# Attention and a two-layer MLP on one core: Winograd's running sums move into PSUM, and the down-projection lags by two periods

## The chip, the cores and the metric

The kernel runs on one core of a Trainium2 chip. The metric is device time of one execution in microseconds (us). Engines are named as in the profile: PE (TensorE), DVE (VectorE), ACT (ScalarE), POOL (GpSimd), SP (SyncE, which issues most DMAs). PEld is PE's weight load.

## The reference

```python
# q, k, v: (8, 8, 576, 64) float32; moe_w_in (512, 2048), moe_w_out (2048, 512)
scores = q @ k.T / 8
# heads 0-3: a query sees the 32 keys up to itself; heads 4-7: every 32nd key up to itself
attn = softmax(where(mask, scores, -1e9)) @ v
x = attn.transpose(0, 2, 1, 3).reshape(4608, 512)
out = (maximum(x @ w_in, 0) ** 2) @ w_out
```

## The kernel before, in words

Every float32 operand of a large matmul is split into a high part h and a rest l (both fp32r), and a product is three matmuls (hh, hl, lh). 4608 tokens are in 12 chunks of 384 (`TC`).

*Attention.* Heads 0-3 ("local") are done chunk by chunk on PE in `pair(c, pr)`: scores s (16 matmuls), minima on DVE (L268), exp on ACT (L275), scaling on ACT and POOL, transposes on DVE (L289), then o (16 matmuls). `STARTS` gives the half step at which each pair of heads begins. Heads 4-7 ("strided") use no PE: in `strided(c)` POOL multiplies (pq, L440; pp, L462) and DVE sums (L441, L463), with two buffers between them, and a softmax between the two halves (L446 to L453); results are transposed by DVE into `ring["s"]`. Their instructions are dealt out over the steps by `PACE` (units of work by step) in `advance`.

*First stage* (to 338 us): chunks 0 to 3 are multiplied plainly by `up` (L499) and `down` (L532), 64 steps. Meanwhile `combos` forms, for each of eight weight pieces p, the seven sums of 256 x 256 weight blocks that Winograd's form of Strassen's scheme needs, split into h and l, and stores them in DRAM (`scr`).

*Second stage*: the other 3072 tokens in six blocks m of 512, eight periods p each, period q = 8m + p. `up7(q)` forms two 128-row tiles of x @ w_in by seven products (1, 7, 2, 6, 4, 3, 5) of a weight sum (tiles ea, eb, streamed from `scr` by `stream`) and an operand op1 to op7 of 256 tokens, six matmuls of 256 columns each (L702). Running sums are kept by accumulating in three PSUM banks u and copying them by ACT to SBUF in between (`keep`, L716); three DVE adds join them into h (L730 to L732), which lies in SBUF. `square(q, h)` squares (L739, L740) and splits them (cast L741; rest L742, one tile on DVE, one on POOL) into g. `down7(q)` multiplies g by w_out into four PSUM banks yy, one for each 128 tokens, 24 matmuls of 512 columns (L758). It runs one period late, but for the last period of a block, whose `down7` runs right away. After it `split_x(m + 1)`, called ahead of that, has rewritten the seven operands from the ring: seven casts on ACT (L675), seven differences (L676; four on DVE, three on POOL) and four sums on DVE (L679, L680, L684, L686), in place in the ring.

The order on each engine is made by a list scheduler at build time, from the order of the code, dependencies and priorities; PE's order is fixed by `on_pe`. Each engine runs its own queue in order.

Of the kernel before, what the change touches and what calls it, by code (L numbers as in the profile page):

```python
# [18 lines left out]
STR = 32  # L19
# [3 lines left out]
P = 128  # L23
# [27 lines left out]
PACE = ((2, 0), (10, 104), (15, 104), (31, 328), (47, 604), (60, 952), (108, 2192), (140, 2812))  # L51

STARTS = {
    2: (8, 12), 3: (16, 20), 4: (22, 24), 5: (26, 28), 6: (32, 34),
    7: (40, 42), 8: (46, 48), 9: (50, 52), 10: (54, 56), 11: (62, 64),
# [62 lines left out]
def attn_moe(ctx: ExitStack, tc, qk_d, v_d, qk_p, v_p, f_s, q_s, k_s, v_s, w_in, w_out, masks, eye, out):  # L118
# [113 lines left out]
    done_to = {"split": 0, "l": 0, "s": 0}  # L232

    def into(kind, c, col, n):

        t0 = TC * (c - NCL) + col
        assert t0 + n - RING <= done_to["split"] <= t0, (kind, c, col, done_to)
        done_to[kind] += n
        return in_ring(c, col, n)


    def pair(c, pr):
# [10 lines left out]
        vr = buf(lpool, "v", 2 * NW * D, "vx", bufs=1)  # L253
        last["s"] = nc.sync.dma_start(out=vr, in_=v_d[c, pr])
# [5 lines left out]
        s_ps = [psum((3 + h) if c <= NCL + 1 else 1 + h, f"s{h}{u}") for h in range(2)]  # L260
        for w in range(NW):
            k0 = TC + wins[w][0]
            for h in range(2):
                rows = slice(D * h, D * (h + 1))
                last["mm"] = nc.tensor.matmul(s_ps[h][:QC, w * kw : (w + 1) * kw], qk[rows, w * QC : (w + 1) * QC], qk[rows, k0 : k0 + kw], start=True, stop=True)
# [6 lines left out]
        yield  # L272
        for h in range(2):
# [29 lines left out]
        else:  # L303
            for a, b, at in into("l", c, 0, TC):
# [110 lines left out]
    def strided(c):  # L415
        for b, i0, i1, col in ranges(c):
# [48 lines left out]
            if c >= NCL:  # L465
                for a in range(2):
                    for n0, n1, at in into("s", c, col, ni * STR):
# [49 lines left out]
    def down(c, j):  # L517
        gh, gl = g_tiles.pop((c, j))
# [10 lines left out]
        for t in range(NTT):  # L529
# [3 lines left out]
        if j == NFT - 1:  # L533
            for t in range(NTT):
# [88 lines left out]
    def combos():  # L623
        for p in range(NPER):
            hi, lo = wi[p]
            for i, at in ((0, 0), (2, 2 * P), (4, 6 * P)):
                nc.sync.dma_start(out=scr[p][:, i], in_=f32(pieces[p][:, :, at : at + 2 * P]))
            full = spare[:, :1024]
            for n, at in enumerate((512, 0)):
                sl = slice(at, at + 512)  # L630
                (nc.gpsimd if n else nc.vector).tensor_add(full[:, sl], f32(hi[:, sl]), f32(lo[:, sl]))
                yield
# [8 lines left out]
            for i, t in ((1, s3), (3, s2), (5, s4), (6, s1)):  # L641
                so = lpool.tile([P, 2, 2 * P], F32R, name=f"so{p}_{i}", tag="so", bufs=1)
                nc.scalar.copy(so[:, 0], t)
                nc.gpsimd.tensor_sub(so[:, 1], t, f32(so[:, 0]))  # L644
                nc.sync.dma_start(out=scr[p][:, i], in_=f32(so))
# [21 lines left out]
    def split_x(m):  # L667
        assert done_to["l"] >= 2 * min(TS * (m + 1), NT - NCL * TC) and done_to["s"] >= TS * (m + 1), (m, done_to)
        v, g = nc.vector, nc.gpsimd
# [3 lines left out]
        def split(nm, src, eng):  # L673
            t = opnd[nm]
            nc.scalar.copy(t[:, 0], src)  # L675
            eng.tensor_sub(t[:, 1], src, f32(t[:, 0]))  # L676

        split("1", b11, v)
        v.tensor_sub(b11, b12, b11)  # L679
        v.tensor_sub(b12, b22, b12)  # L680
        split("7", b12, v)
        split("2", b21, g)
        split("3", b22, v)
        v.tensor_sub(b22, b22, b11)  # L684
        split("6", b22, v)
        v.tensor_sub(b21, b21, b22)  # L686
        split("4", b21, g)
        split("5", b11, g)
        done_to["split"] = TS * (m + 1)
# [6 lines left out]
    def product(acc, e, x, start):  # L696
# [11 lines left out]
    def up7(q):  # L708
        e = entry.pop(q)
        x, y, a = (psum(i, f"u{i}_{q}") for i in range(3))  # L710
        vt = ring["v"]
# [298 lines left out]
```

## Time and profile before

| | |
|---|---|
| median of 3 runs | 950.7 us (950.64 to 954.09) |
| profiled execution, its span | 950.65 us, 948.8 us |
| PE, PEld busy | 93%, 82% |
| DVE, ACT, POOL busy | 72%, 55%, 70% |
| second stage on PE | 338.4 to 944.9 us |
| granted clock, mean | 0.974 |

Busy is the share of the span in which the engine had an instruction under way; it is a mean over stages. A wait is put down to the instruction whose semaphore came last. The chain of work that ended last is followed back from the last instruction.

### The profile page before, as it was taken

The page shows a single profiled execution, that of the slowest core. Times are in us where ns is not written, and L with a number is a line of the kernel's source. Part 1 is how long each engine was busy: PE and PEld are TensorE (multiplying, and loading weights), DVE is VectorE, ACT ScalarE, POOL GpSimd, SP SyncE. Part 2 cuts the span into 40 slices and gives each one's busy share as a digit, 9 for nine tenths or more (in the row PEclk, how much of TensorE's full clock was granted, in tenths as well). Part 3 has the DMA queues.
Part 4 walks back from the last instruction along what each step waited for, and adds up shares of the span by engine and source line. Part 5 has one row for each costly group of instructions (what it writes and reads, how often), then busy time and mean ns, then how long its engine had stood idle before and what let it go on. Part 6 is the DMA issues. An engine that isn't in the chain of part 4 may idle for free.

```text
span 948.8 us, 16167 instructions
## 1 busy us (share of the span) xinstructions
PE 883.6 (93%) x5587; PEld 776.5 (82%) x5587; DVE 682.9 (72%) x1776; ACT 518.5 (55%) x1334; POOL 661.8 (70%) x664
## 2 busy tenths in 40 slices
PE   8999999999999989997999599996999789999998
PEld 7888797887788878886888488885888578888997
DVE  5786779788888878787777977788767977453222
ACT  6998645455555545453655445563644644554443
POOL 3789787878676788797699688877889868321111
PEclk9999999999999999998999799997999899999999
DMA  9986523324264164663656265553755344545441
GB/s 358 389 295 194 191 76 108 115 101 144 89 229 160 37 219 139 210 242 120 225 180 216 103 211 179 197 186 108 236 198 196 109 165 161 196 156 200 159 152 45
DMA packets 46001, 165.93 MB, mean 175 GB/s; under 512 B 4768, under 2 KB 11552, under 8 KB 38240
## 3 DMA queue, kind: packets, MB, share of 16 engines
q1 hardware_dynamic: 45632, 164.58, 49.8%
q8 instruction: 44, 0.72, 0.3%
q10 hardware_dynamic: 288, 0.33, 0.1%
q14 instruction: 37, 0.30, 0.1%
HBM read 140.77 MB, written 24.12 MB: 174 GB/s over the span
## 4 chain that ended last, share of the span: by engine, by line
PE 44%; DVE 21%; POOL 16%; ACT 11%; issue 5%; DMA 3%; ACTq 0%; POOLq 0%; DVEq 0%
PE yy L758 19%; PE u L702 17%; POOL pp L462 5%; POOL pq L440 5%; DVE p_t L289 4%; PE y L532 3%; DVE op L676 3%; DVE sc L441 2%; PE h L499 2%; ACT e L275 2%; DMA scr<-so 2%; POOL w L209 2%; DVE qs L463 1%; POOL so L644 1%; ACT h L739 1%
## 5 line engine op out<-in xcount | busy, mean ns | idle before, releaser
L758 PE MATMUL yy<-w,g 128*128 128x512 f32 x864 | 226.5, 402 | 32.0 <-ACT g L741 21.8
L440 POOL TENSOR_TENSOR pq<-ks,qs 128x512 f32<-128x512 f32 (+2 forms) x192 | 209.1, 1109 | 33.6 <-DVE sc L441 30.0
L462 POOL TENSOR_TENSOR pp<-vs,sc 128x448 f32<-128x448 f32 (+10 forms) x192 | 197.3, 1054 | 47.5 <-DVE qs L463 24.5
L758 PEld LDWEIGHTS yy<-w,g 128*128 128x128 f32 x864 | 162.1, 193 | 70.5 <-ACT g L741 24.0
L499 PE MATMUL h<-x,w 128*128 128x384 f32 x768 | 148.1, 343 | 11.7 <-DVE gl L513 6.8
L702 PE MATMUL u<-op,ea 128*128 128x256 f32 x1152 | 150.3, 285 | 6.9 <-ACT ring L716 5.0
L702 PEld LDWEIGHTS u<-op,ea 128*128 128x128 f32 x1152 | 144.8, 191 | 14.5 <-ACT ring L716 7.5
L716 ACT COPY ring<-u 128x256 f32<-128x256 f32 x192 | 70.5, 371 | 153.5 <-PE u L702 152.1
L441 DVE TENSOR_REDUCE sc<-pq 128x8 f32<-128x512 f32 (+4 forms) x228 | 118.9, 533 | 47.1 <-POOL pq L440 44.8
L499 PEld LDWEIGHTS h<-x,w 128*128 128x128 f32 x768 | 135.2, 190 | 19.3 <-DVE gl L513 10.7
L463 DVE TENSOR_REDUCE qs<-pp 128x64 f32<-128x448 f32 (+11 forms) x192 | 106.5, 564 | 52.8 <-POOL pp L462 51.5
L532 PE MATMUL y<-w,gh 128*128 128x512 f32 x384 | 119.8, 396 | 0.5 <-POOL w L209 0.5
L702 PE MATMUL u<-op,eb 128*128 128x256 f32 x864 | 113.5, 284 | 5.1 <-ACT ring L716 4.7
L702 PEld LDWEIGHTS u<-op,eb 128*128 128x128 f32 x864 | 107.3, 192 | 7.3 <-ACT ring L716 7.3
L739 ACT ACTIVATE h<-h 128x512 f32<-128x512 f32 x96 | 58.9, 632 | 62.8 <-DVE h L731 62.3
L758 PE MATMUL yy<-w,op 128*128 128x512 f32 x288 | 86.0, 409 | 0.0
L532 PEld LDWEIGHTS y<-w,gh 128*128 128x128 f32 x384 | 71.8, 189 | 15.3 <-POOL w L209 0.8
L742 DVE TENSOR_TENSOR g<-h,g 128x512 fp32r<-128x512 f32 x48 | 55.9, 1165 | 36.6 <-ACT g L741 36.3
L742 POOL TENSOR_TENSOR g<-h,g 128x512 fp32r<-128x512 f32 x24 | 32.1, 1339 | 63.1 <-ACT g L741 63.0
L289 DVE STREAM_TRANSPOSE p_t<-e 32x128 f32<-32x128 f32 x240 | 72.1, 300 | 3.9 <-ACT e L281 1.0
L742 POOL TENSOR_TENSOR op<-h,op 128x512 fp32r<-128x512 f32 x24 | 36.3, 1513 | 55.2 <-ACT op L741 49.3
L532 PE MATMUL y<-w,gl 128*128 128x512 f32 x192 | 73.4, 394 | 0.0
(131 smaller groups left out, 1303.8 us busy)
## 6 DMA issues: line engine op xcount, KB each, us to landing
ea<-scr SPq DMA_DIRECT2D x48, 1024.0 KB, 5.1
eb<-scr SPq DMA_DIRECT2D x48, 768.0 KB, 5.9
scr<-so SPq DMA_DIRECT2D x32, 256.0 KB, 2.0
raw<-w_in SPq DMA_DIRECT2D x7, 1024.0 KB, 11.2
v<-v_d SPq DMA_DIRECT2D x24, 256.0 KB, 4.6
scr<-w SPq DMA_DIRECT2D x24, 256.0 KB, 5.7
y<-ysbb SPq DMA_DIRECT2D x24, 256.0 KB, 2.0
vs<-v_s SPq DMA_DIRECT2D x10, 576.0 KB, 4.1
```

Source lines behind the costliest of these rows:

```text
L289: nc.vector.transpose(out=p_t[h][STR * k : STR * (k + 1), :, STR * r : STR * (r + 1)], in_=ev[STR * r : STR * (r + 1), :, STR * k : STR * ...
L440: nc.gpsimd.tensor_mul(pv, kt[:, a : a + m, :], qt[:, i - i0 : i - i0 + 1, :].broadcast_to([P, m, D]))
L441: nc.vector.tensor_reduce(out=sc[:, i - i0, a : a + m], in_=pv, op=ALU.add, axis=AX.X)
L462: nc.gpsimd.tensor_mul(pv, vt[:, a : a + nd, :n], sc[:, il : il + 1, :n].broadcast_to([P, nd, n]))
L463: nc.vector.tensor_reduce(out=ot[:, il, a : a + nd], in_=pv, op=ALU.add, axis=AX.X)
L499: done = nc.tensor.matmul(ph[:, :TC], w[:, wsl], xx, start=n == 0, stop=n == 11)
L532: done = nc.tensor.matmul(y_ps[c][t], g[:, sl], w[:, wsl], start=j == 0 and k == 0, stop=j == NFT - 1 and k == 2)
L702: done = nc.tensor.matmul(acc, w, xx, start=start and n == 0, stop=n == 5, skip_group_check=not start)
L716: nc.scalar.copy(vt[:, i], src[:, :HS])
L739: nc.scalar.activation(h[o], h[o], AF.Relu)
L742: (nc.gpsimd if o else nc.vector).tensor_sub(gl, h[o], f32(gh))
L758: done = nc.tensor.matmul(y_ps[m][t], g[:, sl], w[:, wsl], start=p == 0 and o == k == 0, stop=p == NPER - 1 and o == 1 and k == 2)
```

## The change

Products now run in the order 1, 7, 2, 6, 5, 4, 3 in `period(q, ...)`. ACT copies the running sum x into the bank of h1 (first half, later second half) and of h2 (first half); products 2, 4 and 3 are accumulated by PE on top of what ACT wrote there, with no clearing start. DVE adds only product 7 (v7), once into h2 and once in place into h1. Relu, Square and the cast then work on the PSUM banks, and both rests are DVE's (`finish`). The four token tiles of a down-projection stand between the products: tile 0 behind product 7, tile 1 behind 6, tile 2 behind 4, tile 3 behind 3. They belong to period q - 2, at the ends of blocks too; the first two periods take the last two steps of the first stage, and two down-projections follow the last period. `sums_of_x(m)` forms the four operand sums on POOL into tiles of their own, a period ahead; `split_x(m)` does seven casts (ACT) and seven rests, all on POOL, at high priority.

In `combos` both halves of a weight sum are added by POOL (one was DVE's); the four stored sums rotate over three buffers instead of one, and positions 4 to 6 of `scr` change places. The v of a local pair is loaded after its scores. `PACE` and `STARTS` change by a few numbers.

```diff
-PACE = ((2, 0), (10, 104), (15, 104), (31, 328), (47, 604), (60, 952), (108, 2192), (140, 2812))
+PACE = ((2, 0), (10, 104), (15, 104), (31, 328), (47, 604), (60, 952), (106, 2192), (140, 2812))
-    2: (8, 12), 3: (16, 20), 4: (22, 24), 5: (26, 28), 6: (32, 34),
+    2: (8, 12), 3: (16, 20), 4: (22, 24), 5: (26, 28), 6: (32, 35),
...
 def combos():
-                (nc.gpsimd if n else nc.vector).tensor_add(full[:, sl], f32(hi[:, sl]), f32(lo[:, sl]))
+                nc.gpsimd.tensor_add(full[:, sl], f32(hi[:, sl]), f32(lo[:, sl]))
...
+    def sums_of_x(m):
+        t1, t2 = (pl.tile([P, TS], F32, name=f"t{i}_{m}", tag=tag) for i in (1, 2))
+        t3 = lpool.tile([P, TS], F32, name=f"t3_{m}", tag="so", bufs=1)
...
+        g.tensor_sub(t3, b22, b12)
+        g.tensor_sub(t1, b12, b11)
+        g.tensor_sub(t2, b22, t1)
+        g.tensor_sub(t4, b21, t2)
+        xsum[m] = {"1": b11, "7": t3, "2": b21, "6": t2, "5": t1, "4": t4, "3": b22}
+    def split_x(m):
+        for nm, src in xsum.pop(m).items():
+            t = opnd[nm]
+            with tc.high_priority():
+                nc.scalar.copy(t[:, 0], src)
+                nc.gpsimd.tensor_sub(t[:, 1], src, f32(t[:, 0]))
...
+    def finish(q, half, t):
+        gh, gl = (gs[4 * (q % 2) + 2 * half + i] for i in range(2))
+        nc.scalar.activation(t, t, AF.Relu)
+        nc.scalar.activation(t, t, AF.Square)
+        nc.scalar.copy(gh, t)
+        nc.vector.tensor_sub(gl, t, f32(gh))
+        return gh, gl
+    def period(q, downs, scores, outputs):
+        x, h1 = psum(0, f"x{q}"), psum(1, f"ha{q}")
+        product(first(x), e[0], opnd["1"], True)
+        with hp():
+            nc.scalar.copy(first(h1), first(x))
+        t7 = psum(3, f"t{q}")
+        product(first(t7), e[1], opnd["7"], True)
+        with hp():
+            nc.scalar.copy(v7, first(t7))
+        downs(0)
+        product(first(h1), e[2], opnd["2"])
+        product(first(x), e[3], opnd["6"])
+        with hp():
+            nc.scalar.copy(second(h1), first(x))
+        scores()
+        downs(1)
+        product(first(x), e[4], opnd["5"])
+        product(second(h1), e[5], opnd["4"])
+        h2 = psum(2, f"hb{q}")
+        with hp():
+            nc.scalar.copy(first(h2), first(x))
+            nc.vector.tensor_add(second(h2), first(x), v7)
+            nc.vector.tensor_add(second(h1), second(h1), v7)
+            g1 = finish(q, 0, h1)
+        downs(2)
+        outputs()
+        product(first(h2), e[6], opnd["3"])
+        downs(3)
+        with hp():
+            g2 = finish(q, 1, h2)
...
+    for q in range(NM * NPER + 2):
+        def downs(t, q=q):
+            if q >= 2:
+                down7(q - 2, t)
+            elif t < NTT:
+                on_pe(lambda: down(NCL - 1, NFT - 2 + q, t))
...
+        if p == NPER - 2 and m + 1 < NM:
+            sums_of_x(m + 1)
+        period(q, downs, lambda: scores(k), lambda: outputs(k))
```

How the change moves instructions, at three places. On PE, at the end of the second block (period 15; u are the up-projection's banks, yy1 the block's four output banks, w1_7 the w_out piece of period 15), before:

```order
L702 MATMUL u2_15_6287<-op43_4152,eb15_6066 128x256 x6
L702 MATMUL u0_15_6285<-op5_4153,eb15_6066 128x256 x6
L758 MATMUL yy1_0_5503<-w1_6_1231,g_4154 128x512 x6
L758 MATMUL yy1_1_5504<-w1_6_1231,g_4154 128x512 x6
L758 MATMUL yy1_2_5505<-w1_6_1231,g_4154 128x512 x6
L758 MATMUL yy1_3_5506<-w1_6_1231,g_4154 128x512 x6
L758 MATMUL yy1_0_5503<-w1_7_1282,g_4154 128x512 x3
L758 MATMUL yy1_0_5503<-w1_7_1282,op5_4153 128x512 x3
```

and after (x, t, ha, hb are the banks of the running sum, product 7, h1 and h2):

```order
L714 MATMUL hb15_6388<-op43_4127,eb15_6153 128x256 x6
L778 MATMUL yy1_3_5634<-w1_5_1103,op5_4128 128x512 x6
L714 MATMUL x16_6484<-op17_4125,ea16_6293 128x256 x6
L714 MATMUL t16_6493<-op17_4125,ea16_6293 128x256 x6
L778 MATMUL yy1_0_5631<-w1_6_1231,g_4129 128x512 x6
```

The tiles that need period 15's g (w1_7) stood right behind period 14's; now the next block's products start behind the last tile of period 13.

On DVE, in period 20, around the joining of the sums (sc<-pq are the strided reductions), before:

```order
L441 TENSOR_REDUCE sc9_3_6433<-pq9_3_14_0_6738 128x8
L730 TENSOR_TENSOR h1_20_7062<-u1_20_7059,ring_3198 128x256
L441 TENSOR_REDUCE sc9_3_6433<-pq9_3_14_8_6741 128x7
L731 TENSOR_TENSOR h1_20_7062<-u0_20_7058,ring_3198 128x256
L732 TENSOR_TENSOR h0_20_7061<-u2_20_7060,ring_3198 128x512
L441 TENSOR_REDUCE sc9_3_6433<-pq9_3_15_0_6744 128x8
```

and after:

```order
L443 TENSOR_REDUCE sc9_3_6455<-pq9_3_7_0_6460 128x8
L755 TENSOR_TENSOR hb20_7133<-x20_7079,ring_3182 128x256
L756 TENSOR_TENSOR ha20_7080<-ha20_7080,ring_3182 128x256
L443 TENSOR_REDUCE sc9_3_6455<-pq9_3_8_0_6463 128x8
L443 TENSOR_REDUCE sc9_3_6455<-pq9_3_8_8_6466 128x1
L725 TENSOR_TENSOR g_4129<-ha20_7080,g_4129 128x512
```

Three adds became two, both into PSUM; the strided attention stands about ten reductions further back against the same period.

On POOL, where the operands are rewritten for the fourth block (L742 are rests of g, pp products of the strided attention), before:

```order
L742 TENSOR_TENSOR g_4154<-h1_22_7365,g_4154 128x512
L462 TENSOR_TENSOR pp9_3_12_32_7055<-vs9_3_6429,sc9_3_6433 128x416
L462 TENSOR_TENSOR pp9_3_13_0_7200<-vs9_3_6429,sc9_3_6433 128x448
L462 TENSOR_TENSOR pp9_3_13_32_7203<-vs9_3_6429,sc9_3_6433 128x448
L283 TENSOR_TENSOR e110_0_7439<-e110_0_7439,rs10_0_7441 96x512
L462 TENSOR_TENSOR pp9_3_14_0_7206<-vs9_3_6429,sc9_3_6433 128x480
L676 TENSOR_TENSOR op26_4151<-spare_90,op26_4151 128x512
L462 TENSOR_TENSOR pp9_3_14_32_7209<-vs9_3_6429,sc9_3_6433 128x480
L462 TENSOR_TENSOR pp9_3_15_0_7212<-vs9_3_6429,sc9_3_6433 128x512
L676 TENSOR_TENSOR op5_4153<-ring_3198,op5_4153 128x512
```

and after (L689 to L692 are operand sums, L700 rests of operands):

```order
L464 TENSOR_TENSOR pp9_3_10_32_6946<-vs9_3_6451,sc9_3_6455 128x352
L689 TENSOR_TENSOR t3_3_7333<-spare_90,ring_3182 128x512
L691 TENSOR_TENSOR t2_3_7332<-spare_90,t1_3_7331 128x512
L700 TENSOR_TENSOR op43_4127<-spare_90,op43_4127 128x512
L464 TENSOR_TENSOR pp9_3_11_0_6949<-vs9_3_6451,sc9_3_6455 128x384
L464 TENSOR_TENSOR pp9_3_11_32_6952<-vs9_3_6451,sc9_3_6455 128x384
L700 TENSOR_TENSOR op17_4125<-t3_3_7333,op17_4125 128x512
L692 TENSOR_TENSOR ring_3182<-spare_90,t2_3_7332 128x512
L700 TENSOR_TENSOR op26_4126<-t2_3_7332,op26_4126 128x512
```

The rests of g left POOL; operand sums and all rests of operands came, each block's behind the strided products that complete its tokens. The rewriting begins about seven strided products earlier than it did (ahead of pp9_3_11 instead of behind pp9_3_14).

More of the change, by code (lines that the diff above doesn't have):

```diff
@@ L264, in pair @@
                 rows = slice(D * h, D * (h + 1))
-                last["mm"] = nc.tensor.matmul(s_ps[h][:QC, w * kw : (w + 1) * kw], qk[rows, w * QC : (w + 1) * QC], qk[rows, k0 : k0 + kw], start=True, stop=True)
+                last["mm"] = nc.tensor.matmul(s_ps[h][:QC, w * kw : (w + 1) * kw], qk[rows, w * QC : (w + 1) * QC], qk[rows, k0 : k0 + kw], start=not (late and w), stop=True, skip_group_check=late)
         for h in range(2):
@@ L528, in down @@
         wsl = slice(o * DM, (o + 1) * DM)
-        for t in range(NTT):
+        tiles = range(NTT) if only is None else (only,)
+        for t in tiles:
             sl = slice(t * P, (t + 1) * P)
@@ L694, in on_pe, with product @@
             last["pe"] = mm()
[L696 removed]
+    def product(acc, e, x, start=False):
         def mm():
```

198 lines of the change are left out of this document (79 added, 119 removed).

## The prediction

> **What bounds the kernel now.** I read the head of the page first, then the chain that ended last, then a table by stage.
>
> ```profile
> span 948.8 us, 16167 instructions
> PE 883.6 (93%) x5587; PEld 776.5 (82%) x5587; DVE 682.9 (72%) x1776; ACT 518.5 (55%) x1334; POOL 661.8 (70%) x664
> ```
>
> PE is busy 93%, so the question is where the other 65 us are. The profiled execution took 950.65 us, its span 948.8; the median of the runs is 950.7, so a sum made against the profile holds for the median too. The chain (start, length, what) shows what a down-projection with attention matmuls in it costs (first four rows), and an undisturbed period (last two):
>
> ```profile
> 367.33 1.39 PE yy L758 x6
> 368.72 0.81 PE o L298 x16
> 369.53 1.56 PE s L265 x16
> 371.09 4.31 PE yy L758 x18
> ...
> 397.43 5.03 PE u L702 x42
> 402.46 5.47 PE yy L758 x24
> ```
>
> Seven products take 5.03 us, the four token tiles of a down-projection 5.47: a period is 10.5 us, and an o with an s adds 2.6 (375.40 less 367.33, less 5.47). I cut the second stage at the first product of each block of 512 tokens (eight periods) and asked for the busy time of each engine:
>
> ```profile
> 338.40:442.20 103.80, 94.86 (x593) 82.47 (x592) 82.04 (x184) 52.19 (x134) 85.31 (x79) 0.97 0.55 193
> 442.20:551.00 108.80, 96.94 (x610) 84.36 (x609) 84.90 (x217) 56.60 (x153) 85.32 (x78) 0.94 0.53 181
> 551.00:663.80 112.80, 101.38 (x659) 88.04 (x658) 91.42 (x252) 60.80 (x176) 93.68 (x87) 0.95 0.52 180
> 663.80:767.00 103.20, 93.73 (x594) 82.33 (x594) 81.99 (x183) 52.53 (x132) 89.34 (x81) 0.95 0.50 176
> 767.00:859.60 92.60, 89.19 (x578) 79.40 (x578) 52.38 (x112) 48.12 (x112) 44.67 (x41) 1.00 0.50 174
> 859.60:944.90 85.30, 84.34 (x528) 75.96 (x527) 24.18 (x34) 39.21 (x82) 10.29 (x8) 1.00 0.41 142
> ```
>
> Columns: stretch, its length, then PE, PEld, DVE, ACT, POOL busy, granted clock, DMA. Eight periods are 84 us; the last block takes 85.3, the first four 103 to 113. Together 606.5, against 48 x 10.5 + 12 pairs x 2.6 = 535: 71 us too long. The timeline of PE at the end of the second block shows where:
>
> ```profile
> 539.11 1.22 PE L758 MATMUL yy<-w,g 128*128 128x512 f32 x2 [6.78 <-ACT g L741]
> 543.32 0.80 PE L758 MATMUL yy<-w,g 128*128 128x512 f32 x1 [2.99 <-DVE g L742]
> 543.91 1.48 PE L758 MATMUL yy<-w,op 128*128 128x512 f32 x3
> ...
> 549.59 0.85 PE L758 MATMUL yy<-w,g 128*128 128x512 f32 x3
> ```
>
> The block's last down-projection follows its own up-projection, so PE waits 6.78 + 2.99 us for its operands, and then its groups of three take 1.48 us where they take 0.85 once the clock is back. Over the stage PE's two longest groups of waits are these (engine, line, waited for: us, times, longest):
>
> ```profile
> PE yy L758 <- ACT g L741: 21.8, 5, 6.8
> PE yy L758 <- DVE g L742: 10.2, 6, 3.2
> ```
>
> **The change, part by part.**
>
> *Lag and interleaving.* The down-projection of a block's last period now has the next block's products ahead of it; first periods get tiles between their products. That takes both groups of waits, the slow clock behind them, and the smaller waits of the first periods. If nothing came back, 71 us go: 950.65 - 71 = 879. The last 18 matmuls of the first stage only move (no gain). At the end two down-projections remain instead of one: PE's work is the same sum.
>
> *Running sums in PSUM.* Four ACT copies of 256 columns stay four; their target becomes PSUM for three. Relu, Square and the cast are as many as before. The trace shows no copy from PSUM to PSUM. ACT is 51% busy in the stage (sum of its column), and a copy has a tile of 1.39 us beside it before its result is wanted; VectorE's 256-column add out of PSUM takes 0.42 us. Were the copy as long as that add or twice as long, the tile would still cover it: 0 us; without the tile each of three copies would cost its 0.4, some 60 us over 48 periods. PE's matmuls keep shape and count. Eight clearing matmuls cost under 1 us (42 products of 256 columns take 5.03).
>
> *VectorE ahead of the last product.* New: product 3 writes the bank into which VectorE adds x + v7, and waits for that add. From the end of P5 it has product 4 (0.72 us) and one tile (1.37), so 2.1 us; copy and add need some 0.9, which leaves 1.2 for a late VectorE. I took how late it came before from the 48 adds of L731: at best 0.44 us after the last product; first and last of the strided periods inside a block in which it came over 1.2 later still:
>
> ```profile
> 378.11 2.32 PE L702 MATMUL u<-op,eb 128*128 128x256 f32 x18
> ...
> 791.02 2.32 PE L702 MATMUL u<-op,eb 128*128 128x256 f32 x18
> ```
>
> ```profile
> 382.33 0.41 DVE L731 TENSOR_TENSOR h<-u,ring 128x256 f32<-128x256 f32 x1
> ...
> 795.37 0.42 DVE L731 TENSOR_TENSOR h<-u,ring 128x256 f32<-128x256 f32 x1
> ```
>
> There the add starts 1.90 and 2.03 after the product's end. Fourteen such periods exceed the 1.2 us by 13 us together; none of it cost anything before, since a whole down-projection lay behind. Bounds: 0 (VectorE has less to do) to 35 (with the five ends of blocks, where split_x held VectorE). I take 13.
>
> The Trainium skill, PSUM — Partial Sum Buffer, section on bank collisions, states why a write into the other half of the bank is waited for at all: the compiler back end orders any two instructions of different engines on one bank and partitions. No run here shows it; it speaks against this change, and by it the cost is the 13 us above, by separate halves 0.
>
> In the 12 periods with scores, ACT's eight exps can stand ahead of the copy into that bank:
>
> ```profile
> L275 ACT ACTIVATE e<-e,nm 96x128 f32<-96x128 f32 x96 | 37.6, 395 | 0.0
> ```
>
> Eight take 3.2 us, the cover is 2.1. Bounds 0 and 12 x 1.5 = 18 us; I take half of the 1.1 that stick out, 12 x 0.55, about 6.
>
> *VectorE's load.* Durations (min/median/max):
>
> ```profile
> L732 DVE TENSOR_TENSOR h<-u,ring x48: 674/681/683, 344.6 to 934.7; 128x512 f32<-128x512 f32 x48
> L742 DVE TENSOR_TENSOR g<-h,g x48: 677/1184/2716, 352.3 to 938.1; 128x512 fp32r<-128x512 f32 x48
> ```
>
> Before, a period held two adds of 256 columns (0.42 by the rows of L731), L732 and L742, 0.84 + 0.68 + 1.18 = 2.7 us; now two adds of 256 and two differences of 512 with a PSUM input. These I price by L732, the same shape with a PSUM input: 0.84 + 1.36 = 2.2. By L742 instead it would be 3.2. The four differences and four sums per block of split_x leave VectorE for POOL. So VectorE gets lighter, which is why I do not take 35 above.
>
> The Trainium skill, GPSIMD Engine Reference, key points, says GpSimd shares its SBUF interfaces with VectorE and contends with two-SBUF-input instructions there. The trace agrees: L742 with two SBUF inputs spreads from 677 to 2716 ns, L732 with one in PSUM stays at 674 to 683. By the rule the differences cost 0.68, without it 1.18.
>
> *POOL's queue.* It carries the strided attention, which each block's operands need. Its work (second-last group of the row), and its waits, between two strided instructions that stand in both orders (at 299.4, and at 735.3 near the end of block four); the second row is the first stage:
>
> ```profile
> 299.40:735.30 435.90, 400.94 (x2542) 350.75 (x2542) 342.92 (x849) 226.32 (x607) 359.12 (x332) 0.96 0.51 177
> 100.00:338.40 238.40, 227.91 (x1300) 199.88 (x1299) 193.28 (x571) 123.35 (x370) 182.21 (x209) 0.99 0.36 119
> ```
>
> ```profile
> POOL pq L440 <- DVE sc L441: 24.9, 26, 4.1
> POOL pp L462 <- issue: 19.9, 5, 6.6
> POOL pp L462 <- DVE qs L463: 14.8, 17, 4.1
> POOL op L742 <- PE yy L758: 5.8, 1, 5.8
> POOL op L742 <- ACT op L741: 5.6, 1, 5.6
> POOL op L676 <- ACT op L675: 3.0, 1, 3.0
> ```
>
> Busy 359 us, waiting 75. Between the same marks of the new order 30 differences of L742 and 12 of L676 leave, and 28 operand differences and 17 sums come, all of one shape; in the first stage eight adds come. Their rows (tile g; the adds' line):
>
> ```profile
> L742 POOL TENSOR_TENSOR g<-h,g x24: 1269/1293/1759, 349.2 to 927.2; 128x512 fp32r<-128x512 f32 x24
> ```
>
> ```profile
> L631 POOL TENSOR_TENSOR spare<-w x8: 1267/1286/1295, 106.8 to 231.6; 128x512 f32<-128x512 f32 x8
> ```
>
> 42 leave and 45 come: +4 us at one price of 1.29; -4 if the old ones, which met VectorE's differences, cost 0.17 more each. I take 0. The adds are 8 x 1.29 = 10 us; POOL idles 56 of 238 us there, so 0 to 10; I take 10. So POOL has as much to do, and what it can win is its 75 us of waiting. I count as gone the 14.4 behind ACT and PE (L742 and L676 leave POOL) and 18 at the ends of blocks, where VectorE was in split_x: eight waits, of which the first and the last are
>
> ```profile
> 430.37 2.84 POOL L440 TENSOR_TENSOR pq<-ks,qs 128x512 f32<-128x512 f32 x2 [2.15 <-DVE sc L441]
> ...
> 664.00 2.83 POOL L440 TENSOR_TENSOR pq<-ks,qs 128x512 f32<-128x512 f32 x3 [0.73 <-DVE qs L463]
> ```
>
> Together 32. The new order writes operand 7 of block five eight instructions after the 735.3 mark, 9 us. It is ready at 735 + 10 + 9 - 32 = 722. From product 7 of that block to the end PE needs 83.3 + 84, an s and two o (3.4), two lagged down-projections (10.9), and the 5.8 us that now follow the last matmul (944.86 to 950.65): 187. That gives 909; no wait gone 941; all gone 866, under PE's own 879.
>
> At the start of the stage eleven operand instructions stand among sixteen strided products, some 32 us from about 310 (299.4 + 10) on; P4 wants its operand 6.3 us after the stage's start, which moves 4 us ahead to 334, so at 341. 0 to 8 us, I take 4.
>
> *Rest.* The weights of products 4, 5 and 3 are released 9.1 us into a period instead of 5.0, and wanted 17 us later; the load lands in 5.9 us:
>
> ```profile
> eb<-scr SPq DMA_DIRECT2D x48, 768.0 KB, 5.9
> ```
>
> So 0. v is loaded a step later and used two periods on; PACE and STARTS reorder the same 270 strided products: 0 each.
>
> **Sum.** By PE's route 879 + 13 + 6 + 4 = 902; by POOL's 909. The two are so near that waits of one do not quite hide in the other; I take the later: 910.
>
> **Rivals.**
> - PE alone bounds: POOL runs nearly without waits and VectorE is never late; 879 to 893. For it: POOL's waits are mostly on VectorE, which gets lighter. Against: its softmax waits (19.9) have nothing to do with the change.
> - POOL keeps its waits, which only change their cause (it now waits for ACT's casts, which wait for PE): 925 to 941. For it: seven differences per block stand behind casts in its queue.
> - Slower: VectorE is late in every period, and product 3 waits in each. Inside blocks the add started 1.6 us after the product on average (30 strided periods); to eat 71 us in 35 strided periods it must cost 2 us in each, so start 3.3 us or more after: twice as late as now. VectorE's load speaks against it. Price then 955 to 975.
> - No change: both of the last two at half strength, 946 to 955.
>
> **How the numbers follow.** My case (893 to 925) 0.53, PE alone 0.17, POOL keeps its waits (925 to 946) 0.20, no change 0.05, slower 0.05. 886 to 938 leaves out about two tenths. Half a per cent, 4.8 us, is about what can be told from no change here; by the cases faster 0.90, same 0.05, slower 0.05.
>
> **What would show it.** Right: blocks of 90 to 98 us instead of 103 to 113, no wait of a yy matmul for g, the clock near 1.0 at block ends, VectorE's g differences at 0.68 us, POOL's busy time in the stage as before with less waiting; what waits are left on PE are products on POOL's operand differences (blocks four and five) and on the add into the h bank. Wrong: product 3 waiting over 2 us in most periods, or POOL's waits still 75 us to the same mark.

## The result, and the profile after

| | before | after |
|---|---|---|
| median | 951.0 us (950.64 to 954.09) | 923.8 us (920.88 to 925.78) |
| ratio | | 0.9704, 95% interval 0.967 to 0.9739 |
| profiled execution, its span | 950.65, 948.8 | 925.78, 924.0 |
| second stage on PE | 338.4 to 944.9 | 336.2 to 919.9 |

Faster by 27 us; 910 was predicted, 886 to 938 the range. The head of the page after:

```profile
PE 875.2 (95%) x5595; PEld 768.8 (83%) x5595; DVE 602.1 (65%) x1720; ACT 518.9 (56%) x1334; POOL 643.1 (70%) x672
```

DVE has 81 us less to do, POOL 19 less, PE nearly the same. The stage cut again at the first product of each block (columns as before: stretch, length, PE, PEld, DVE, ACT, POOL busy, clock, DMA):

```profile
336.20:432.50 96.30, 88.86 (x578) 77.20 (x579) 71.00 (x207) 53.91 (x151) 78.39 (x78) 0.96 0.58 196
432.50:529.50 97.00, 94.11 (x642) 82.05 (x641) 69.22 (x200) 57.27 (x156) 78.05 (x77) 1.00 0.63 206
529.50:628.80 99.30, 93.92 (x610) 81.89 (x609) 70.48 (x205) 54.37 (x152) 72.37 (x72) 0.98 0.60 199
628.80:733.10 104.30, 92.81 (x593) 81.39 (x592) 70.55 (x183) 52.27 (x134) 90.25 (x90) 0.95 0.53 176
733.10:824.80 91.70, 88.81 (x578) 78.38 (x578) 50.18 (x119) 49.41 (x115) 64.07 (x61) 1.00 0.54 176
824.80:919.90 95.10, 95.10 (x576) 85.03 (x575) 20.64 (x37) 41.42 (x86) 1.29 (x1) 1.00 0.42 141
```

Blocks two and three fell from 108.8 and 112.8 us to 97.0 and 99.3, about as forecast (90 to 98). Block four didn't: 104.3, with the clock at 0.95. What the first block lost and the last one gained is mostly moved work: with a lag of two, the first has 18 matmuls of the first stage (about 4 us) in place of two of its down-projections (10.9 us), and the last has two more. Together 583.7, 22.8 less than the 606.5 of before. PE's groups of waits in the stage (engine, tile, line, waited for: us, times, longest):

```profile
PE ha L714 <- ACT ha L738: 14.3, 13, 3.8
PE t L714 <- POOL op L700: 5.9, 2, 4.3
PE t L714 <- ACT op L699: 5.0, 1, 5.0
PE hb L714 <- DVE hb L755: 3.5, 7, 0.8
PE x L714 <- DVE gl L515: 2.4, 1, 2.4
PE x L714 <- POOL op L700: 1.1, 1, 1.1
```

No yy matmul waits for g any more. The longest group is one that the prediction had at nothing: product 2 waits for ACT's copy into h1's bank. Next are 12.0 us for operands (casts and rests), 9.3 of them at the start of block four and 2.7 in block five. Behind the wait in block four six yy matmuls took 2.76 us, twice their undisturbed time (24 take 5.47). The rows there on PE's timeline:

```profile
634.65 0.58 PE L714 MATMUL t<-op,ea 128*128 128x256 f32 x1 [5.02 <-ACT op L699]
639.53 1.44 PE L714 MATMUL t<-op,ea 128*128 128x256 f32 x5 [4.30 <-POOL op L700]
```

Operand 7's cast and rest wait for the operand sum on POOL (L689), which stands in POOL's queue behind strided products. So I looked at POOL between the two marks of the prediction. The first row is the stretch, the rest are its waits:

```profile
306.50:731.60 425.10, 395.56 (x2566) 345.48 (x2565) 300.09 (x838) 232.50 (x629) 346.12 (x339) 0.98 0.56 184
```

```profile
POOL pp L464 <- DVE qs L465: 25.7, 22, 3.7
POOL pq L442 <- DVE sc L443: 25.2, 27, 3.4
POOL pp L464 <- issue: 15.8, 4, 5.3
POOL op L700 <- ACT op L699: 5.3, 3, 2.7
```

POOL is idle for 425.1 - 346.1 = 79 us; before it was 435.9 - 359.1 = 77. I had counted 32 of them as gone. POOL's waits for PE and ACT ahead of rests fell from 14.4 us to 5.3 and the softmax group ("issue") from 19.9 to 15.8, but the waits for DVE's strided sums grew from 40 to 51, and small ones from 1 to 6. What DVE itself waited for in the same stretch, apart from POOL's products, after and then before:

```profile
DVE g L725 <- ACT g L724: 13.7, 18, 1.7
DVE hb L755 <- ACT hb L754: 13.7, 12, 3.9
DVE e L268 <- PE s L265: 11.1, 6, 3.7
DVE op L725 <- ACT op L724: 8.2, 5, 3.4
```

```profile
DVE ysbb L766 <- PE yy L758: 5.7, 6, 2.6
DVE rs L277 <- ACT e L275: 4.0, 5, 1.6
DVE h L730 <- PE u L702: 3.3, 5, 1.0
DVE g L742 <- ACT g L741: 3.3, 9, 0.5
```

The first four are 47 us, the second four 16; all of DVE's waits for PE and ACT are 56 us after and 22 before. DVE is less busy, but now it stands longer waiting for PE and ACT, at high priority, with strided sums behind. Whether that is what holds POOL up is a question for the experiments.

### The profile page after: what moved, and what is told of

The parts are those of the page before. It is cut to its first block, busy times and chain, and to the rows that moved or that the text cites. A ratio compares the mean times of both kernels' runs of the same rounds, so it can differ in the third digit from the quotient of the medians.

```text
span 924.0 us, 16176 instructions
## 1 busy us (share of the span) xinstructions
PE 875.2 (95%) x5595; PEld 768.8 (83%) x5595; DVE 602.1 (65%) x1720; ACT 518.9 (56%) x1334; POOL 643.1 (70%) x672
## 4 chain that ended last, share of the span: by engine, by line
PE 47%; DVE 19%; POOL 17%; ACT 8%; issue 5%; DMA 4%; SPq 0%; ACTq 0%; POOLq 0%; DVEq 0%
PE yy L778 21%; PE x L714 9%; PE ha L714 6%; POOL pq L442 6%; DVE p_t L291 5%; POOL pp L464 4%; PE hb L714 3%; PE t L714 3%; DVE e L268 2%; DVE sc L443 2%; DMA y<-ysbb 2%; PE h L501 2%; POOL w L209 2%; DVE qs L465 2%; PE y L535 1%
## 5 line engine op out<-in xcount | busy, mean ns | idle before, releaser
L714 PE MATMUL x<-op,ea 128*128 128x256 f32 x576 | 85.8, 285 | 3.4 <-DVE gl L515 2.4
L714 PEld LDWEIGHTS x<-op,ea 128*128 128x128 f32 x576 | 79.9, 194 | 7.6 <-DVE gl L515 2.5
L277 ACT ACTIVATE e<-e,nm 96x128 f32<-96x128 f32 x160 | 62.2, 390 | 22.8 <-DVE nm L268 22.8
L747 ACT COPY ha<-x 128x256 f32<-128x256 f32 x48 | 17.1, 357 | 101.7 <-PE x L714 101.2
L778 PE MATMUL yy<-w,op 128*128 128x512 f32 x288 | 74.2, 393 | 0.0
L755 DVE TENSOR_TENSOR hb<-x,ring 128x256 f32<-128x256 f32 x48 | 20.4, 426 | 68.9 <-ACT hb L754 68.9
L714 PEld LDWEIGHTS ha<-op,ea 128*128 128x128 f32 x288 | 41.2, 195 | 22.9 <-ACT ha L738 19.8
L714 PE MATMUL ha<-op,ea 128*128 128x256 f32 x288 | 44.7, 293 | 14.3 <-ACT ha L738 14.3
L778 PEld LDWEIGHTS yy<-w,op 128*128 128x128 f32 x288 | 51.2, 189 | 8.5
L725 DVE TENSOR_TENSOR g<-ha,g 128x512 fp32r<-128x512 f32 x48 | 33.1, 691 | 32.3 <-ACT g L724 31.9
```

The lines of the kernel that those rows point to most:

```text
L277: nc.scalar.activation(e4[h][:, w], e4[h][:, w], AF.Exp, bias=nm[:QC, h, w : w + 1], scale=-1.0, accum_out=ss[:QC, NW * h + w, :1])
L714: done = nc.tensor.matmul(acc, w, xx, start=start and n == 0, stop=n == 5, skip_group_check=not start)
L725: nc.vector.tensor_sub(gl, t, f32(gh))
L755: nc.vector.tensor_add(second(h2), first(x), v7)
L778: done = nc.tensor.matmul(y_ps[m][t], g[:, sl], w[:, wsl], start=p == 0 and o == k == 0, stop=p == NPER - 1 and o == 1 and k == 2)
```

## The experiments

All are ratios to the kernel before, run on the same chip beside it. The scheduler makes its order anew for each edit. Except in the run on pace, the order on POOL, DVE and ACT differs in every run from that of the kernel it starts from, so a run tests its edit together with the order that came with it. PE's order stays, or all but stays, where the edit isn't about it.

**The lag alone**, without PSUM sums, without tiles between the products and without operand sums on POOL: in the kernel before, `down7` runs one period late at the ends of blocks too.

```diff
-        if p:
+        if q:
             down7(q - 1, event)
...
-        if p == NPER - 1:
+        if q == NM * NPER - 1:
             down7(q)
```

> The kernel before with only the lag made even: down7 runs one period late at the ends of blocks too (the next block's products stand ahead of it); sums stay in SBUF, split_x where it was. If the early down-projection is the whole cost of a block's end: 32 us of waits and 10 of slow clock go, 908 to 914. If split_x, which stands at the same place, takes its place as the wait (in the second block its last operand was written 9 us after the last product): 3 to 5 us for each block, 926 to 936.

926.6 us, ratio 0.9737 (0.9711 to 0.9762), the second of the two cases: the lag alone gives 24 us, where the whole change gives 27. The intervals of the two ratios overlap, so what the rest of the change adds can't be told from nothing by the times. PE's waits for operands in this run:

```profile
PE u L702 <- DVE op L676: 5.9, 5, 2.1
PE u L702 <- ACT op L675: 5.9, 3, 3.0
PE u L702 <- POOL op L676: 4.5, 3, 2.9
```

The 32 us of waits for g are gone (0.5 left), and 16 us of waits for operands have come: the rewriting of the operands is next in line.

**Without the strided attention.** In the second stage's chunks the strided products, sums and softmax are left out, in both kernels; the same edit. (Theory O in the expectation is the one spelled out under Pace below: POOL waits because of the order in DVE's queue.)

```diff
                     m = min(JH, n - a)
+                    if c >= NCL:
+                        yield m
+                        continue
...
```

> The changed kernel without the strided products, sums and softmax for the chunks of the second stage (their loads and transposes stay; that part of the output is not computed). What is left is PE's own route. By theory O: 924 less 12 us of waits for operands less some 4 us of slow clock, 904 to 910. If late VectorE work also causes the waits for the copy into the h1 bank (14 us) and for the add (3.5): 888 to 896.

897.8 us, ratio 0.9434 (0.9403 to 0.9466), between the two ranges. PE then waits 7.4 us for h1's bank, 2.8 for h2's, and for no operand.

> The kernel before with the same part left out. Of its 71 us over 535 us of PE work, what the ends of blocks cost without any strided work stays: by block five, which had little of it, 5 us at each of five ends, and some 10 at the stage's start: 912 to 920 us. If the strided work had no part in the 71 us: 945 to 951.

913.4 us, ratio 0.9605 (0.958 to 0.963), as expected. Without strided work the change is worth 15.6 us. PE's waits for g, which the lag takes away, were 12.6 us in it:

```profile
PE yy L769 <- ACT g L752: 7.9, 5, 2.1
PE yy L769 <- DVE g L753: 4.7, 5, 1.5
```

The strided work costs the kernel before 37 us and the kernel after 26, though it uses no PE: these hang on POOL and DVE.

**Pace.** The strided units are asked for sooner (step 100 instead of 106 for the same amount).

```diff
-PACE = (..., (60, 952), (106, 2192), (140, 2812))
+PACE = (..., (60, 952), (100, 2192), (140, 2812))
```

> The changed kernel with one number changed: PACE gives out the strided attention's units up to 2192 by step 100 instead of 106, so its instructions stand earlier in the queues of DVE and POOL. Theory O (order): POOL still waits 77 us in the stage because DVE's queue holds strided reductions behind events of PE and ACT, and blocks four and five start late only because the strided products stand too far back; then the 12 us of waits for operand 7 and 6 there go, with the slow clock behind them: 906 to 914 us. Rival C (capacity): POOL is simply full; products that stand earlier do not run earlier: 920 to 928 us. Before: 951; changed kernel: 924.

923.3 us, ratio 0.9702 (0.9675 to 0.9728): nothing. The order of instructions came out the same on PE, DVE, ACT and POOL, by names and shapes from the first to the last. The edit moved nothing, so the run tests neither theory; that its time is in the rival's range says nothing for the rival.

**Four buffers for the strided products.** If DVE's late sums hold POOL up through two buffers, more buffers should free it without any change in work.

```diff
+    def product_tile(c, name):
+        if c >= 6 and next(turn) % 2:
+            return gpool.tile([P, JH * D], F32, name=name, tag="gl")
+        return spool.tile([P, JH * D], F32, name=name, tag="prod", bufs=2)
...
-                    prod = spool.tile([P, JH * D], F32, name=f"pq{u}_{i}_{a}", tag="prod", bufs=2)
+                    prod = product_tile(c, f"pq{u}_{i}_{a}")
...
```

> The strided products of GpSimd get four buffers instead of two (from the seventh chunk on every other product goes into the buffers that held the first stage's rests of g); the work is the same. My theory: GpSimd's 51 us of waits for VectorE's strided sums come from the sums standing in VectorE's queue behind adds and differences that wait for TensorE and ScalarE, with only two products in flight. With four the two waits together fall under 25 us, the operands of blocks four and five are ready at least 10 us sooner, TensorE's waits for rests and casts of operands (12 us) go, and the time is 910 to 917 us. Rival one, VectorE's or GpSimd's own work is what is full: the waits move or stay, 921 to 926 us. Rival two, products that run more often beside VectorE's sums get longer by contention: the waits fall, the products' mean rises from 1.29 us to 1.4 or more, 918 to 926 us.

926.3 us, ratio 0.9728 (0.9707 to 0.9749). No gain, but a flawed test. One new wait on PE stands just ahead of the stage:

```profile
PE clear L939 <- DVE gl L522: 22.7, 1, 22.7
```

The borrowed buffers were still those of the first stage, and its last rests (gl) had to wait for strided sums. The second stage began at 357.0 us instead of 336.2; from the first to the last x product that reads tile ea it took 546.5 us instead of 566.6. So it was run again from the eighth chunk on, when the first stage is over:

```diff
-        if c >= 6 and next(turn) % 2:
+        if c >= 7 and next(turn) % 2:
```

> Again four buffers for GpSimd's strided products, but from the eighth chunk on, so that the first stage's buffers of g aren't touched before it ends (with the seventh chunk the second stage began at 357.0 us instead of 336.2 and then took 20 us less). If the few buffers set GpSimd's pace, the second stage begins at 334 to 338 us, GpSimd's waits for VectorE's strided sums fall from 51 us to under 25, TensorE's 12 us of waits for operands go and the time is 912 to 918 us: about what the kernel with four rests on VectorE takes (914.9), since TensorE's waits for the copies into h1's bank then set the time. Rival: the 20 us were the late start, in which GpSimd ran ahead: 921 to 926 us.

907.7 us, ratio 0.9536 (0.9518 to 0.9554): 16 us faster than the kernel after, with as many instructions on each engine, and the stage begins at 334.7. POOL's waits up to 740 us (the three largest of those for softmax and sums), then DVE's, then PE's in the stage:

```profile
POOL pp L471 <- issue: 20.6, 4, 6.0
POOL pq L449 <- DVE sc L450: 7.7, 13, 1.6
POOL pp L471 <- DVE qs L472: 7.2, 5, 2.7
```

```profile
DVE hb L762 <- ACT hb L761: 21.9, 14, 2.8
DVE g L732 <- ACT g L731: 21.5, 23, 1.7
```

```profile
PE ha L721 <- ACT ha L745: 7.0, 8, 3.8
PE ha L721 <- POOL op L707: 4.9, 1, 4.9
PE hb L721 <- DVE hb L762: 2.9, 5, 1.5
```

DVE waits for ACT no less than before (43 us in these two groups, 27 in the kernel after), yet POOL's waits for its sums fell from 51 to 15 us. The first rest of block five's operands starts at 708.6 instead of 722.6. Between the prediction's two marks (the same two strided products in every run) POOL is idle 50 us, where it was 77 and 79 in the kernels before and after.

This run alone doesn't tell the buffers from the new order, but all of them together nearly do. Between these marks POOL was idle 71 to 80 us in seven kernels with two buffers (before, after, lag, pace, fewer rests, no exps, and these two together), though their orders differ, but for pace, and DVE waited anything from 16 to 56 us for PE and ACT. In the three with four buffers it was idle 47 to 50 us, and DVE waited 48 to 62. So it is not how long DVE is held up that counts, but that POOL could be only two products ahead of it. (The kernel with the tiles behind the products, two buffers, has 65 us, but its PE takes a quarter longer.)

**No sums.** DVE's sums over the strided products are left out in the second stage's chunks.

```diff
-                    nc.vector.tensor_reduce(out=sc[:, i - i0, a : a + m], in_=pv, op=ALU.add, axis=AX.X)
+                    if c < NCL:
+                        nc.vector.tensor_reduce(out=sc[:, i - i0, a : a + m], in_=pv, op=ALU.add, axis=AX.X)
```

> VectorE's sums over the strided products are left out in the second stage's chunks (some 390 instructions); GpSimd's products stay, so the output is another. My theory (the products wait for VectorE's queue): GpSimd has no wait for these sums, all its marks come 50 us or more sooner, no wait of TensorE for operands is left, and the time is near that of the kernel without any strided work (897.8 us): 896 to 905 us. Rival (GpSimd's own 1.3 us instructions fill it): operands of block five still come after 725 us and the time is 915 to 924 us.

943.7 us, ratio 0.9918 (0.9893 to 0.9942): both theories missed the time. The scheduler, with other work to place, also made another order of the first stage, and the second began at 359.6 us instead of 336.2. From there to the end it took 584.7 us, only 3 less than in the kernel after; PE waited in it 12.2 us for an add into h2's bank and 6.8 for a copy into h1's. What my theory said of POOL came true: no wait for sums was left, PE waited for no operand, and POOL's second mark came at 680.6 instead of 731.6. POOL took 390 us between its marks, much as with four buffers (388), and waited for ACT's copies and casts instead (32 and 14 us up to 740). The late start alone is 23 us of the time, and what made the two long waits on PE isn't known, so the time doesn't decide between the theories.

**Fewer rests on POOL.** DVE takes four of the seven rests of operands.

```diff
-                nc.gpsimd.tensor_sub(t[:, 1], src, f32(t[:, 0]))
+                (nc.vector if nm in "1736" else nc.gpsimd).tensor_sub(t[:, 1], src, f32(t[:, 0]))
```

> The rests of four of the seven operands of each block are taken by VectorE instead of GpSimd (24 instructions of 1.3 us leave GpSimd's queue, 24 of 0.7 to 1.3 us come to VectorE's). If GpSimd's own work sets when the operands of blocks four and five are ready (rival), they come 20 us or more sooner and the time is 908 to 915 us. My theory, GpSimd goes at the pace of VectorE's queue: VectorE gets 17 to 30 us more ahead of the strided sums, GpSimd's waits for them grow by about as much as its work shrinks, and the time is 919 to 927 us; the last wait then is for a rest on VectorE.

914.9 us, ratio 0.9613 (0.9591 to 0.9636): the rival's figure. My theory said that POOL's waits would grow by what its work shrank; they did not:

```profile
POOL pq L442 <- DVE sc L443: 25.5, 28, 4.1
POOL pp L464 <- DVE qs L465: 18.3, 19, 2.5
POOL pq L442 <- DVE qs L465: 7.4, 4, 3.2
```

51.2 us for sums up to 740 us, as in the kernel after. POOL's busy time fell from 643 to 620 us. Between the marks its work fell from 346 to 329 us, its idle time from 79 to 75, and the second mark came 25 us sooner; the operand waits on PE vanished. So what counts is the sum of POOL's work and its waits up to a block's rewriting, and cutting either helps. Only 9 of the 25 us reach the time, since PE then waits for h1's and h2's banks (16.0 and 5.9 us).

**ACT's exps.** The exponentials of the local pairs are left out from chunk 6 on, counted from 0 (the seventh; the expectations call it the sixth).

```diff
-            for w in range(NW):
+            for w in range(NW if c <= NCL + 1 else 0):
                 nc.scalar.activation(e4[h][:, w], e4[h][:, w], AF.Exp, ...)
```

> ScalarE's exponentials of the local score pairs are left out from the sixth chunk on (the maxima, sums and products with the unexponentiated scores stay; the output is another). My theory: TensorE's waits for the copy into h1's bank (14.3 us, of which 3.8 at the stage's start) and for the add into h2's (3.5 us) stand behind these exponentials in ScalarE's queue: without them 14.3 becomes 5 or less, 3.5 becomes 1.5 or less, and the time is 911 to 917 us. Rival: the copies are late because of the g rests and Relu, Square of the period before, which stay: the waits keep more than 10 us and the time is 920 to 924 us.

926.0 us, ratio 0.9724 (0.9699 to 0.9749): no gain. PE's waits show it given back:

```profile
PE t L714 <- ACT op L699: 8.9, 2, 8.7
PE t L714 <- POOL op L700: 8.9, 2, 4.6
PE hb L714 <- DVE hb L755: 8.0, 9, 1.7
PE ha L714 <- ACT ha L738: 7.1, 6, 3.6
```

The waits for h1's bank halved (14.3 to 7.1), but those for operands grew from 12.0 to 17.8, and those for h2's bank, which should have shrunk too, from 3.5 to 8.0. PE came to block four 9.5 us earlier (619.3 against 628.8), while POOL's second mark stayed (730.5 against 731.6). Here a shorter wait inside the periods was given back, as POOL's operands set when a block may start. To see what such waits cost otherwise, both edits together:

```diff
-                nc.gpsimd.tensor_sub(t[:, 1], src, f32(t[:, 0]))
+                (nc.vector if nm in "1736" else nc.gpsimd).tensor_sub(t[:, 1], src, f32(t[:, 0]))
...
-            for w in range(NW):
+            for w in range(NW if c <= NCL + 1 else 0):
```

> Four of the seven rests on VectorE, and ScalarE's exponentials of the local pairs left out from the sixth chunk on (the output is another). Alone the first gave 914.9 us and the second nothing (926.0: TensorE waited 7 us less for the copy into h1's bank and 7 us more for operands). My theory: with the operands early, the exponentials are what makes the copies into h1's and h2's banks late, so the waits for them fall from 16.0 and 5.9 us to under 6 and under 3, and the time to 899 to 906 us. Rival: the copies wait for Relu, Square and the casts of the period before, which stay: 911 to 916 us.

911.0 us, ratio 0.958 (0.955 to 0.961): 4 us less than with the rests alone, though the intervals overlap, and the rival's figure. PE waits 6.9 us for h1's bank instead of 16.0, but 9.1 instead of 5.9 for h2's and 3.7 for operands. The exps, with the order that came without them, are somewhat over half of the first wait, and taking them away doesn't give it all back.

**Tiles behind the products.** All four token tiles stand behind product 3. One thing more changes by it: tiles 0 and 1 now come after `finish` has written the same buffers of g, so they multiply the g of their own period, with no lag.

```diff
-        downs(0)
         product(first(h1), e[2], opnd["2"])
...
-        downs(3)
+        for t in range(4):
+            downs(t)
```

> All four token tiles of the down-projection stand behind product 3 instead of between the products; copies, sums and the lag of two stay. If the tiles are what covers the copies, a period shows the copy after product 6 (0.36 us and a hand-over on each side), and the copy and the add ahead of product 3 (0.36 + 0.43 and hand-overs): 1.0 to 2.0 us in each of 48 periods, less where scores stand between: 965 to 1010 us, slower than the kernel before the change. Rival: ScalarE's and VectorE's queues set when the copies are done, not the cover: 921 to 935 us.

1151.7 us, ratio 1.2105 (1.2075 to 1.2135). Both theories missed, since the run undid half of the lag as well:

```profile
PE yy L776 <- ACT g L724: 104.3, 46, 3.9
PE hb L714 <- DVE hb L753: 23.9, 39, 1.8
PE x L714 <- ACT ha L746: 16.1, 36, 0.4
```

The first row is the lost lag; with 18.2 us more for DVE's rests of g it is 2.6 us a period. The other two are, as far as this run can show it, what the tiles cover: 0.61 us for the add into h2's bank and 0.45 for the copy ahead of product 5 each time, 40 us in all. How much of it a run with the whole lag would show is open. PE's own busy time rose too, from 875 to 964 us: yy matmuls that read g took 478 ns instead of 396, at a granted clock of 0.927 in the mean instead of 0.983.

**The best two together.** Four buffers as in the second of those runs, and the rests of operands 7 and 4 on DVE.

```diff
-                nc.gpsimd.tensor_sub(t[:, 1], src, f32(t[:, 0]))
+                (nc.vector if nm in "74" else nc.gpsimd).tensor_sub(t[:, 1], src, f32(t[:, 0]))
```

> The four buffers of the run before (907.7 us), and the rests of operands 7 and 4 on VectorE (12 instructions). TensorE still waited 5.6 us for GpSimd's rests there (4.9 for operand 4, 0.7 for operand 7), 7.0 for copies into h1's bank and 2.9 for the add into h2's. If those 5.6 us are simply to be had: 901 to 905 us. Rival: 12 more instructions in VectorE's queue, or strided sums that get in ahead of the adds now, give them back as waits for h1's and h2's banks: 906 to 912 us.

911.7 us, ratio 0.9576 (0.955 to 0.9602): the rival's figure, 4 us slower than four buffers alone (the intervals just touch). The operand waits went, but

```profile
PE ha L721 <- ACT ha L745: 11.0, 8, 4.8
PE hb L721 <- DVE hb L762: 7.7, 5, 3.3
```

grew by 8.8 us. For the longest of the second row, 3.3 us at 717.2, the trace shows the cause: one of the twelve rests, both inputs in SBUF, took 4.84 us, seven times the shortest (0.68), while POOL ran four instructions without a pause, and the add that PE waits for came behind it in DVE's queue.

```profile
709.87 4.84 DVE L707 TENSOR_TENSOR op<-t,op 128x512 fp32r<-128x512 f32 x1
```

The longer waits of the first row (at 351, 388 and 509 us) stand far from any of the twelve; there the cause is open, and the order had changed too. The best version is the one with four buffers, 907.7 us.

## Why the prediction was right, and where it was not

*The lag* (71 us gone): its mechanism was right. The waits for g went, and the lag alone gave 24 us. But 71 was all that PE lost, and the waits for g were 32 of it; with the lag alone, 16 us of waits for operands came in their place.

*POOL's route* is the step that failed. I put operand 7 of block five at 735 + 10 + 9 - 32 = 722; PE's product 7 there got its rest at 735.7, after waiting 1.6 us for it. The 10 were 7.1 (306.5 against 299.4). The 9 from the mark to the rest were 4.1: four instructions, not eight. The 32 us of waits were not won: 77 became 79. Of the 14.4 that should have left with the rests, 5.3 came back, since the new rests of operands wait for ACT's casts too. I had assumed that a wait behind an engine goes when that engine has less to do. DVE had less to do, but its waits for ACT and PE rose from 22 to 56 us, and POOL, two buffers ahead at most, waited as long as before. The runs point to the two buffers as the cause; the rise of DVE's waits isn't shown to be one, since in the run without exps DVE's waits for PE and ACT fell from 56 to 40 us and POOL stayed idle for 80. What the prediction priced at 0, POOL's work, shrank by 13 us (359.1 to 346.1), since the old instructions of 512 columns had cost 1.31 to 1.56 us in the mean and cost 1.27 to 1.30 now. The way from product 7 to the end, 187 in the sum, took 190.

So the time fell into the range of my own case (893 to 925) partly by luck: 13 us less of POOL's work and 8 less in the other two terms, none of it in the sum, made up for most of the waits that stayed. By mechanism the rival "POOL keeps its waits, which only change their cause" was nearer (925 to 946, with a chance of 0.20 against my 0.53), though the cause that it names, ACT's casts, is 5.3 us only. The mark that I had set for being wrong, POOL's waits still 75 us, was met. The sum's price for these waits was about right: with four buffers 29 us of them went, and the time was 907.7, near the sum's 909.

*PE's route*, term by term: the add and the exps ahead of product 3, 13 and 6, cost 3.5 us together (DVE was lighter, as argued against the higher bound). Product 3 writes the first half of the bank and the add the second, so the 3.5 us also show that in this program a matmul into one half of a bank waits for an add into the other, as the Trainium skill says (PSUM — Partial Sum Buffer, bank collisions). The copies, priced at 0, cost 14.3 at h1's bank. The tile does cover the copy's own 0.36 us. What I overlooked is that the copy needs h1's bank, and this is released only when DVE has read it for the rest of g, a period later. So it was in nine of the thirteen waits (11.3 us); in the other four the copy followed right behind one of ACT's own casts. ACT's and PE's rows at 725 us:

```profile
724.89 0.36 ACT L738 COPY ha<-x 128x256 f32<-128x256 f32 x1 [1.57 <-DVE g L725]
```

```profile
725.30 0.98 PE L714 MATMUL ha<-op,ea 128*128 128x256 f32 x6 [1.29 <-ACT ha L738]
```

The stage's start cost 2.4 us (a rest of the first stage) and 3.8 (the second period's copy, counted above), not the 4 for operand 4. So PE's sum would be 879 + 14.3 + 3.5 + 2.4 = 899 against the 902 forecast. The operand waits, 12.0, bring it to 911. PE's busy time in the stage is 553.6 us (sum of the column), where 535 and 4.1 for the 18 first-stage matmuls in it (by 24 in 5.47) were to be had: 14.5 us of longer matmuls bring it to 925.7, and the profiled execution took 925.8.

*DVE's prices* held: the rests of g took 0.69 us where 0.68 was forecast and 1.18 was the other value.

```profile
L725 DVE TENSOR_TENSOR g<-ha,g x48: 680/692/693, 352.2 to 908.3; 128x512 fp32r<-128x512 f32 x48
```

*What the PSUM sums are worth* isn't shown by a run of their own. In the kernel as it is, the whole change gains 27 us and the lag alone 24. Without strided work the whole change gains 15.6 us, and the waits for g that the lag takes are 12.6. Both leave some 3 us for PSUM sums, tiles and operand sums together.

## What to carry to other kernels

When work moves to PSUM and becomes a step that waits on the matmuls, ask which in-order queue it now heads and who is fed from behind it: an engine with less to do can still keep its neighbour waiting as long. A wait between two engines may be cured by depth instead of by work: two more buffers, with the order that the scheduler made for them, gave 16 us here, where moving rests to another engine gave 9 and taking exponentials away gave nothing. And a bank that is reused each period is a dependency of its own: look for its last reader before a copy is priced at nothing.

## What the runs showed of the hardware

GpSimd's own instructions got shorter when VectorE's differences had one input in PSUM instead of both in SBUF. The same strided products of 512 columns, before and after:

```profile
L440 POOL TENSOR_TENSOR pq<-ks,qs 128x512 f32<-128x512 f32 x81 | 108.6, 1352 | 19.6 <-DVE sc L441 18.4 <-DVE qs L463 0.7
```

```profile
L442 POOL TENSOR_TENSOR pq<-ks,qs 128x512 f32<-128x512 f32 x82 | 105.0, 1292 | 24.2 <-DVE sc L443 19.9 <-DVE rs L279 2.0 <-DVE qs L465 1.4
```

1352 to 1292 ns in the mean. The trace of the kernel before shows it within one run. Between the two marks, 57 of GpSimd's 512-column instructions overlapped one of VectorE's differences or sums of operands and g, with both inputs in SBUF; they took 1508 ns in the mean and up to 1841. The 83 others took 1284, and none over 1308. In the kernel after, no such overlap is left, and none of the 157 from 300 to 745 us took over 1345. With four rests on VectorE again it is back: 19 overlapping ones took 1453 in the mean, 126 others 1286. It works the other way too: VectorE's rest of 4.84 us above, and one of 4.55 us in the run with four rests there. The size I had not expected: 13 us of POOL's time over the stretch. That GpSimd and VectorE contend for their shared access to SBUF is what the Trainium skill says (GPSIMD Engine Reference, key points), and these rows agree.
